# Polynomial attention and expert block on one core: first query rows in a second queue, their first factor ahead of the key projection, a shorter decode, 1e-6 added by a product, and eight warm-up matmuls for ten

## Chip, cores, metric

One core of one Trainium2 chip. The metric is the device time of one execution in microseconds (us). All quoted runs of the program on its one core are in the state called fast; a single core shows no die to compare.

In the profile's lines the first number is the start in us and the second the length. PE is TensorE's matmuls and PEld its weight loads, DVE is VectorE, ACT ScalarE, POOL GpSimd and SP SyncE; a q behind a name marks an instruction of that engine's sequencer, such as the issue of a transfer. `out<-in` names the tiles, L193 a line of the kernel, and a bracket the idle time before and what ended it.

## The reference, cut to what matters

```python
q, k, v: (4, 4, 1088, 32) float32;  S1, S2: (8, 32) float64
phi(x) = outer(S1 x, S2 x)                  # 64 features
kv = phi(k)^T v;   z = sum(phi(k))
attn = (phi(q) kv) / (phi(q) z + 1e-6)      # -> x (4352, 128)
p = domain_probs / (sum(domain_probs) + 1e-9)
out = sum_e p[:, e] * relu(x @ w1[e]) @ w2[e]   # 4 experts, 1024 wide
```

The expert block is nearly all of the work. The attention of the first 128 rows has to be ready before it can begin; the rest of the attention is fed in between its products.

## The kernel before: the parts that matter

S1 and S2 are 64-bit floats, decoded by integer operations on VectorE. Then `start()` makes the first 128 rows of x as fast as it can. Cuts are marked.

```python
load_rows(k, 0, "kn")                     # 544 KB, SyncE
load_rows(q, 0, "qn", slice(0, P))        # 64 KB, SyncE
vn[0] = load_v(0)                         # six transfers, SyncE
...
keep_warm(10)                             # products of zeros
... # words: 14 operations, then the transpose into s_T
... # ScalarE: four copies sk<-s_T; GpSimd: three sp<-s_T, four sr<-sp
def start():
    for r in range(3): key_turn(b, r)     # VectorE: kT
    qT = query_turn(b, 0, n)              # VectorE
    key_project(b, 0..2)                  # PE: sk x kT, 72 instructions
    for i in range(3): ...                # PE: factors sr[i] x qT, 24
    ...                                   # products, key sums (72), kvz
    first = attend_first(b, 0, n, qp)     # den, num; then the division
```

Later rows of x take another way: VectorE makes a tile, SyncE writes it to DRAM in four transfers (`xd<-y`) and, after waiting for these, reads it back transposed (`xT<-xd`).

## Time and profile before

| | before |
|---|---|
| time, three first runs | 491.32 us median (491.18 to 491.34); a fourth, beside the changed kernel, 491.93 |
| time, 30 further runs beside the experiments | 491.16 to 492.34, mean 491.66 |
| span of the profiled run | 489.5 us |
| first matmul of the expert block (h<-xT) | 14.16 us |

The prediction shows the lines of the page, of the chain and of VectorE's timeline.

### The profile page before, as it was taken

Reading aid. Unit: us, or ns where it says so; the run is one execution under the profiler, and the core shown is the slowest. Engines: PE = TensorE matmul, PEld = TensorE weight load, DVE = VectorE, ACT = ScalarE, POOL = GpSimd, SP = SyncE. Lnnn points to the kernel's source line nnn. Section 1 sums busy time; section 2 is a strip of 40 time slices with the busy share of each in tenths; the row PEclk is TensorE's granted clock in tenths of the full one; section 3 lists DMA queues with packets and bytes.
Section 4 is the critical chain, followed back from the end, with each engine's and each line's share of the span. In section 5 each row is a group of like instructions: output and inputs, shape, how many; then the busy total and the mean of one; then the engine's idle time right before and its main releaser. Section 6 shows DMA issues by size and latency. Waiting matters only on the chain.

```text
span 489.5 us, 11439 instructions
## 1 busy us (share of the span) xinstructions
PE 482.6 (99%) x4602; PEld 361.1 (74%) x4602; DVE 318.5 (65%) x746; ACT 244.4 (50%) x487; POOL 226.8 (46%) x260
## 2 busy tenths in 40 slices
PE   8999999999999999999999999999999999999997
PEld 5877777777767777555777777777777777878997
DVE  6759585868676757768675564575575666665642
ACT  3344463455445634535455464445455455566651
POOL 6052473516355444334555353444555355555570
PEclk9999999999999999999999999999999999999999
DMA  7990230040102520041102200031101200120000
GB/s 207 290 284 22 88 95 1 2 137 1 34 2 80 139 55 1 1 118 23 33 2 87 50 0 1 2 87 23 33 1 55 49 1 1 50 50 2 15 3 18
DMA packets 37588, 26.25 MB, mean 54 GB/s; under 512 B 26016, under 2 KB 34592, under 8 KB 37024
## 3 DMA queue, kind: packets, MB, share of 16 engines
q1 hardware_dynamic: 37520, 25.53, 19.0%
q8 instruction: 36, 0.59, 0.5%
q14 instruction: 16, 0.13, 0.1%
q10 hardware_dynamic: 16, 0.00, 0.0%
HBM read 21.28 MB, written 4.24 MB: 52 GB/s over the span
## 4 chain that ended last, share of the span: by engine, by line
PE 96%; DVE 2%; DMA 1%; issue 0%; ACT 0%; SPq 0%; DVEq 0%
PE h L188 49%; PE o L188 40%; PE f L188 4%; PE den L188 3%; DMA kn<-in_k_dram 1%; DVE qp L450 1%; DVE hid L698 1%; PE num L188 1%; PE h L176 0%; DVE kT L314 0%; ACT hid L723 0%; DVE qa L584 0%; ACT sh L842 0%; SPq L119 0%; DVE xT L486 0%
## 5 line engine op out<-in xcount | busy, mean ns | idle before, releaser
L188 PE MATMUL h<-xT,w_sb 128*64 128x512 f32 (+4 forms) x1408 | 300.2, 495 | 0.5 <-DVE xT L486 0.5
L698 DVE SCALAR_TENSOR_TENSOR hid<-h,hid 128x256 f32<-128x256 f32 (+6 forms) x432 | 203.6, 472 | 148.2 <-ACT hid L723 139.2
L723 ACT ACTIVATE hid<-h 128x512 f32<-128x512 f32 (+3 forms) x288 | 158.4, 550 | 195.0 <-PE h L188 157.0
L188 PE MATMUL o<-hid,w2s 128*64 128x256 f32 (+3 forms) x1152 | 221.6, 355 | 0.0
L188 PE MATMUL o<-hid,w_sb 128*64 128x256 f32 (+3 forms) x864 | 183.9, 355 | 0.0
L188 PEld LDWEIGHTS h<-xT,w_sb 128*64 128x64 f32 x1408 | 144.2, 137 | 51.8 <-issue 9.2
L188 PEld LDWEIGHTS o<-hid,w2s 128*64 128x64 f32 x1152 | 131.7, 137 | 30.9 <-issue 0.2
L838 POOL TENSOR_TENSOR ev<-yz,sh 64x256 f32<-64x256 f32 (+3 forms) x72 | 48.4, 672 | 163.5 <-ACT sh L841 160.8
L188 PEld LDWEIGHTS o<-hid,w_sb 128*64 128x64 f32 x864 | 101.0, 137 | 24.5 <-issue 6.3
L826 POOL TENSOR_TENSOR yz<-ev 128x512 f32<-128x512 f32 (+3 forms) x36 | 42.1, 1170 | 61.8 <-ACT ev L829 61.8
L838 POOL TENSOR_TENSOR ct<-ev 128x512 f32<-128x512 f32 (+3 forms) x36 | 42.0, 1167 | 2.8
L838 POOL TENSOR_TENSOR ct<-ct,gate 128x512 f32<-128x512 f32 (+3 forms) x27 | 32.1, 1189 | 2.1
L838 POOL TENSOR_TENSOR total<-total,ct 128x512 f32<-128x512 f32 (+3 forms) x27 | 31.8, 1179 | 2.1
L450 DVE TENSOR_TENSOR qp<-qa,qb 64x384 f32<-64x384 f32 (+3 forms) x44 | 32.1, 729 | 1.0
L828 ACT COPY ev<-o 128x512 f32<-128x512 f32 (+3 forms) x36 | 19.4, 539 | 11.3 <-PE o L188 10.8
L188 PE MATMUL o<-w_sb,hid 128*64 128x128 f32 x256 | 21.7, 273 | 0.0
L829 ACT COPY ev<-o 128x512 f32<-128x512 f32 (+3 forms) x36 | 19.4, 539 | 2.6
L715 ACT ACTIVATE hid<-h 128x256 f32<-128x256 f32 x24 | 9.2, 384 | 21.2 <-PE h L188 20.7
L188 PEld LDWEIGHTS o<-w_sb,hid 128*64 128x64 f32 x256 | 17.8, 137 | 2.1 <-issue 1.9
L353 DVE TENSOR_TENSOR kp<-fs 128x256 f32<-128x256 f32 (+1 forms) x24 | 14.7, 617 | 0.0
L841 ACT COPY sh<-yz 64x256 f32<-64x256 f32 (+3 forms) x36 | 13.7, 379 | 1.7 <-POOL yz L826 0.8
L842 ACT COPY sh<-yz 64x256 f32<-64x256 f32 (+3 forms) x36 | 13.7, 380 | 0.9
(113 smaller groups left out, 230.2 us busy)
## 6 DMA issues: line engine op xcount, KB each, us to landing
w_sb<-in_moe_w_dram SPq DMA_DIRECT2D x8, 512.0 KB, 7.5
gate<-gates SPq DMA_DIRECT2D x4, 1024.0 KB, 5.5
kn<-in_k_dram SPq DMA_DIRECT2D x4, 544.0 KB, 4.6
vn<-in_v_dram SPq DMA_DIRECT2D x16, 128.0 KB, 4.2
gate<-gates SPq DMA_DIRECT2D x2, 896.0 KB, 5.7
qn<-in_q_dram SPq DMA_DIRECT2D x3, 544.0 KB, 5.5
xd<-y SPq DMA_DIRECT2D x26, 48.0 KB, 1.7
out_dram<-ob SPq DMA_DIRECT2D x16, 64.0 KB, 2.0
```

Of the source, the lines that this page charges most:

```text
L188: nc.tensor.matmul(out(s), weights(s), moving(s), **flags)
L353: eng.tensor_tensor(out=_ap(kps[b], 0, P, 256 * t0 + P * p + 64 * x, [[256, n], [32, 2], [R, 4], [1, R]]), in0=_ap(src, 0, P, off + 4 * x, ...
L450: nc.vector.tensor_tensor(out=qp[p][64 * x : 64 * x + 64, 0:n], in0=qa[64 * p : 64 * p + 64, 0:n], in1=qb[64 * p : 64 * p + 64, 0:n], op=A ...
L698: nc.vector.scalar_tensor_tensor(out=out, in0=src, scalar=0.0, in1=in1, op0=ALU.max, op1=ALU.subtract)
L715: nc.scalar.activation(hd[:, 0 : 2 * n], hp[:, 0 : 2 * n], ACTF.Relu)
L723: nc.scalar.activation(hd[:, n * j : n * j + n], hp[:, 0:n], ACTF.Relu)
L826: add = lambda out, in0, in1, op=ALU.add: nc.gpsimd.tensor_tensor(out=out, in0=in0, in1=in1, op=op)
L828: nc.scalar.copy(_ap(ev, 0, P, 0, [[2 * w, 2], [1, w]]), _ap(a0, 0, P, 0, two))
L829: nc.scalar.copy(_ap(ev, 0, P, w, [[2 * w, 2], [1, w]]), _ap(a1, 0, P, 0, two))
L838: add = lambda out, in0, in1, op=ALU.add: nc.gpsimd.tensor_tensor(out=out, in0=in0, in1=in1, op=op)
L841: nc.scalar.copy(sh[HP:P, 0:w], yz[0:HP, 0, 0:w])
L842: nc.scalar.copy(sh[0:HP, 0:w], yz[HP:P, 1, 0:w])
```

## The change

Intent: fill the PE's wait for the keys with the first of three query factors, for which q's rows and the decoded words must come earlier; shorten the division by one operation. Two of the ten warm-up matmuls, products of zeros that raise the PE's clock, are dropped as well.

```diff
-    load_rows(q, 0, "qn", slice(0, P))
+    load_rows(q, 0, "qn", slice(0, P), nc.scalar)
...
-    keep_warm(10)
+    keep_warm(8)
... # words: shift and OR in one operation (scalar_tensor_tensor), 14 -> 12
... # copies: factor i = sp[i] on GpSimd, sr[i] two on ScalarE, two on GpSimd;
    # order: factors(0), sk (two and two), factors(1), factors(2)
@@ attend_first
+        if c == 0:
+            for _ in range(2):
+                on_side(den, ones of vx, eps, start=True, stop=False)   # 1e-6
...
-                    start=True,
+                    start=(i > 0 or c > 0),
...
-        rc = dT * 1.0 + 1e-6 ; reciprocal(rc)
+        reciprocal(rc, dT)                                    # for c == 0
@@ start
+        qT = query_turn(b, 0, n)          # before the keys
         for r in range(3):
             key_turn(b, r)
-        qT = query_turn(b, 0, n)
+        factor(0)
         key_project ...                   # second copy fs before the first of vx
+        factor(1)
+        factor(2)
```

More of the change, by code (lines that the diff above doesn't have):

```diff
@@ L84, in psum, with load_rows @@
         return pool.tile([P, 512], F32, tag=tag, name=tag)
-    def load_rows(src, b, name, part=slice(0, S)):
+    def load_rows(src, b, name, part=slice(0, S), engine=nc.sync):
         d = kn if name == "kn" else qn
@@ L92, in load_rows @@
         c, n = part.start, part.stop - part.start
-        nc.sync.dma_start(d[b][:, part], bass.AP(src.tensor, src.offset + b * H * S * D + c, [[G * D, P], [1, n]]))
+        engine.dma_start(d[b][:, part], bass.AP(src.tensor, src.offset + b * H * S * D + c, [[G * D, P], [1, n]]))
     def load_v(b):
@@ L170 @@
         nc.gpsimd.memset(own2[32 * h : 32 * h + 32, h % 2 : h % 2 + 1], 1.0)
+    eps = cpool.tile([P, 1], F32, name="eps")
+    nc.gpsimd.memset(eps[:, :], 0.0)
+    nc.gpsimd.memset(eps[0:1, :], 1e-6)
     def keep_warm(n):
@@ L200, in bits, with either @@
         nc.vector.tensor_scalar(out=out, in0=in0, scalar1=s1, scalar2=s2, op0=op0, op1=op1)
-    def either(out, a, b):
-        nc.vector.tensor_tensor(out=out, in0=a, in1=b, op=ALU.bitwise_or)
+    def either(out, in0, s1, op0, in1):
+        nc.vector.scalar_tensor_tensor(out=out, in0=in0, scalar=s1, in1=in1, op0=op0, op1=ALU.bitwise_or)
     low = _ap(s_raw, 0, R2, 0, [[2, D]])
@@ L214, with copy_on, factors @@
     bits(s_m[:, lo], high, 31, shr, 31, shl)
+    bits(s_x[:, hi], high, 12, shl, 9, shr)
     bits(s_e[:, hi], s_f[:, hi], float(127 - 1023), ALU.add, 0.0, ALU.max)
     bits(s_e[:, lo], s_f[:, hi], float(127 - 1023 - 52), ALU.add, 0.0, ALU.max)
-    bits(s_x[:, hi], high, 12, shl, 9, shr)
-    bits(s_x[:, lo], low, 29, shr)
-    bits(s_n[:, hi], s_e[:, hi], 1.0, ALU.min)
+    either(s_x[:, hi], low, 29, shr, s_x[:, hi])
     bits(s_n[:, lo], low, 3, shl, 3, shr)
     bits(s_f[:, :], s_e[:, :], 255.0, ALU.min)
-    either(s_x[:, hi], s_x[:, hi], s_x[:, lo])
-    bits(s_e[:, :], s_f[:, :], 23, shl)
-    either(s_m[:, hi], s_x[:, hi], s_m[:, lo])
-    either(s_f[:, :], s_e[:, :], s_m[:, :])
+    either(s_m[:, hi], s_m[:, lo], 0, shl, s_x[:, hi])
+    bits(s_n[:, hi], s_e[:, hi], 1.0, ALU.min)
+    either(s_f[:, :], s_f[:, :], 23, shl, s_m[:, :])
     nc.vector.tensor_tensor(out=s_hl[0:R2, :], in0=s_n[:, :], in1=s_f[:, :].bitcast(F32), op=ALU.mult)
     nc.vector.transpose(s_T[:, :], s_hl[:, :])
-    for h in range(H):
-        nc.scalar.copy(_ap(sk, 32 * h, 32, R2 * h, [[HP, 2], [1, R2]]), _ap(s_T, 0, 32, 0, [[D, 2], [1, R2]]))
-    for i in range(3):
-        nc.gpsimd.tensor_copy(
+    def copy_on(scalar):
+        return nc.scalar.copy if scalar else nc.gpsimd.tensor_copy
+    def factors(i):
+        copy_on(False)(
             _ap(sp, 0, 32, HP * i, [[32, 2], [R, 4], [1, R]]),
@@ L239 @@
         )
+        for h in range(H):
+            copy_on(h < 2)(
+                _ap(sr, 32 * h, 32, 2 * P * i + 32 * h, [[P, 2], [1, 32]]), _ap(sp, 0, 32, HP * i, [[32, 2], [1, 32]])
+            )
+    factors(0)
     for h in range(H):
-        nc.gpsimd.tensor_copy(
-            _ap(sr, 32 * h, 32, 32 * h, [[P, 6], [1, 32]]), _ap(sp, 0, 32, 0, [[32, 6], [1, 32]])
-        )
+        copy_on(h < 2)(_ap(sk, 32 * h, 32, R2 * h, [[HP, 2], [1, R2]]), _ap(s_T, 0, 32, 0, [[D, 2], [1, R2]]))
+    factors(1)
+    factors(2)
     mask_lo = [R2 + l % R2 for l in range(32)]
@@ L460, in attend_first @@
         nd = [psum(ps_n, "den"), psum(ps_n, "num")]
+        if c == 0:
+            for _ in range(2):
+                on_side(
+                    lambda s: nd[0][half[s], 0:n],
+                    lambda s: _ap(vx, 0, P, D, [[0, HP]]),
+                    lambda s: _ap(eps, 0, P, 0, [[0, n]]),
+                    start=True,
+                    stop=False,
+                )
         for i in range(2):
@@ L474, in attend_first @@
         rc = apool.tile([P, QW // 32], F32, tag="rc", name="rc")
-        nc.vector.tensor_scalar(
-            out=rc[:, 0 : n // 32], in0=_ap(dT, 0, P, 0, [[32, n // 32]]), scalar1=1e-6, scalar2=1.0, op0=ALU.add, op1=ALU.mult
-        )
-        nc.vector.reciprocal(rc[:, 0 : n // 32], rc[:, 0 : n // 32])
+        column = _ap(dT, 0, P, 0, [[32, n // 32]])
+        if c:
+            nc.vector.tensor_scalar(
+                out=rc[:, 0 : n // 32], in0=column, scalar1=1e-6, scalar2=1.0, op0=ALU.add, op1=ALU.mult
+            )
+            column = rc[:, 0 : n // 32]
+        nc.vector.reciprocal(rc[:, 0 : n // 32], column)
         rb = apool.tile([P, UNITS[0][1]], F32, tag="rb", name="rb")
@@ L613, in start, with factor @@
         b, n = 0, UNITS[0][0]
-        kf = []
+        qT = query_turn(b, 0, n)
+        fq = [psum(ps_o, "o0"), psum(ps_o, "o1"), psum(ps_n, "num")]
+        def factor(i):
+            for j in range(2):
+                both(fq[i][:, 0:n], sr[:, i, j, :], qT[:, 0:n], start=(j == 0), stop=(j == 1))
         for r in range(3):
             key_turn(b, r)
-        qT = query_turn(b, 0, n)
-        for gi in range(3):
-            kf.append(psum(ps_h, "h"))
+        factor(0)
+        kf = [psum(ps_h, "h") for _ in range(3)]
         value = value_copy(b)
         key_project(b, 0, kf[0])
+        key_project(b, 1, kf[1])
         next(value)
-        key_project(b, 1, kf[1])
         key_project(b, 2, kf[2])
@@ L626, in start @@
             pass
-        fq = [psum(ps_o, "o0"), psum(ps_o, "o1"), psum(ps_n, "num")]
-        for i in range(3):
-            for j in range(2):
-                both(fq[i][:, 0:n], sr[:, i, j, :], qT[:, 0:n], start=(j == 0), stop=(j == 1))
+        factor(1)
+        factor(2)
         qb = apool.tile([P, QW], F32, tag="qb", name="qb")
```

## The prediction

> **What bounds the kernel now.** I read the page first, its busy shares, its line of tenths and its chain, then the waits of the PE, then the chain in order of time for the first 16 us, and last the timeline of each engine over that stretch.
>
> ```profile
> span 489.5 us, 11439 instructions
> PE 482.6 (99%) x4602; PEld 361.1 (74%) x4602; DVE 318.5 (65%) x746; ACT 244.4 (50%) x487; POOL 226.8 (46%) x260
> PE   8999999999999999999999999999999999999997
> ```
>
> The PE is busy 99% of the span and only its first and last slices (12.2 us each) have gaps. From 14.2 us on, the waits of the PE name one wait on another engine, 0.6 us in total, and the stretches 14.16 to 40 us show the PE busy for 25.84 of 25.84 us. So two things follow. What this change can win lies before 14.16 us, where the main part's first real matmul starts. And what is won there should reach the end nearly whole, since nothing after it waits for a fixed date such as a weight load: no wait of the PE names one.
>
> The front part, in the chain in order of time:
>
> ```profile
> 1.21 3.73 DMA kn<-in_k_dram
> ...
> 4.96 0.72 DVE kT L314
> 5.68 0.14 issue
> 5.82 2.32 PE h L188 x72
> 8.14 0.88 PE o L188 x16
> 9.01 0.44 PE num L188 x8
> 9.45 2.12 PE f L188 x72
> ...
> 11.66 0.30 DVE kvz L376
> 11.96 0.04 issue
> 12.01 0.44 PE den L188 x4
> ...
> 13.68 0.40 DVE xT L486
> ```
>
> The key rows land at 4.94 us, VectorE turns them (kT), the PE projects the keys (72 instructions), then makes the three query factors (16 + 8 instructions, 1.32 us), then the key sums (72), all without a gap. Then comes a string of small steps: kvz, den, and on VectorE the division, shown by its timeline:
>
> ```profile
> 12.49 0.32 DVE L472 STREAM_TRANSPOSE dT<-den 128x128 f32<-128x128 f32 x1 [0.35 <-PE den L188]
> 12.85 0.17 DVE L475 TENSOR_SCALAR rc<-dT 128x4 f32<-128x4 f32 x1
> 13.05 0.18 DVE L478 RECIPROCAL rc<-rc 128x4 f32<-128x4 f32 x1
> ```
>
> The word operations that decode S1 and S2 are **not** on this chain: they end with the transpose into s_T at 4.44 us and VectorE then stands 0.52 us until the keys land. ScalarE has sk ready at 5.44 us, the first kT is there at 5.65 us.
>
> **What the Trainium skill says.** (1) "DMA: Bandwidth & Descriptors", section "Issuing engines are not separate DMA queues": transfers of all issuers run on the same 16 engines and interleave; another issuer saves only issue time. The trace agrees with the saving: one issue on SyncE takes about 0.43 us. It also warns me: today q's 64 KB stand behind the 544 KB of keys in one queue, with a second queue they move among them. (2) "VectorE: DVE Perf Modes", section on the fixed extra latency of operations whose source is in SBUF: a small operation costs a fixed amount, not by size. The trace agrees: 16x32 words take 0.16 to 0.17 us each, 16x64 take 0.18, and independent ones start 0.09 us apart, dependent ones 0.21 to 0.25. (3) "TensorE: Matmul & The Clock Gate", Part 1: the array runs at half clock until a free-running window of about 3.4 us was busy. In the trace the warm-up matmuls start 0.43 us apart until the eighth at 4.16 us and the ninth follows after 0.30 us, so the clock came up near 4.3 us, inside the eighth. (4) "PSUM — Partial Sum Buffer", the four PSUM rules: a matmul without the starting flag adds onto what the group's first one wrote. So the 1e-6 can come in as a first product. No row of the kernel before shows that use.
>
> **The change, part by part.**
>
> *q's rows by ScalarE's queue.* ScalarE's first issue ends near 1.32 us, so q is issued at about 1.35 instead of 1.62. ScalarE's table load (1.28 us) moves back by some 0.43 us to end near 3.1; ScalarE is idle until 4.54, so this is free. SyncE's later issues, v above all, come 0.43 us earlier. Before, ScalarE waited 0.39 us for v at 7.77, so that wait goes. The price: q's 64 KB now compete with the keys. At the rate of the busiest half microsecond there (418 GB/s) 64 KB are 0.16 us. I estimate that the keys land 0.1 us later, between 0 and 0.3, at about 5.05.
>
> *The words.* Fourteen operations become twelve. Following starts, 2.47 us for the first, 0.09 each for the independent ones, about 0.25 for the last three dependent steps, I get the end of s_T at about 4.16 instead of 4.44: 0.28 us. None of it is on the path by itself; it pays for the next part.
>
> *The copies.* GpSimd's sp(0) runs 4.23 to 4.46 (0.23 as now). Then two sr copies on each of ScalarE and GpSimd, of 32x64, at the 0.17 to 0.23 us spacing that the sp and sk copies show: sr(0) is ready at about 5.0. The two sk copies per engine follow: ready at about 5.45, as today. The rest, sp(1), sp(2) and four sr copies on each engine, end near 6.7 on both, before ScalarE is needed for fs (7.01 before).
>
> *Factor 0 in front.* Eight of the 24 factor instructions leave the middle. By the chain 24 cost 1.32 us, so eight cost 0.44. In front, they need q turned. VectorE now turns q first (0.27 us for 128x128, of which the next operation sees some 0.1 to 0.2), as soon as q lands, which I put close to the keys. Then kT begins at about 5.15 rather than 4.96, ends at about 5.85, and the keys' projection starts at about **6.0** instead of 5.82. Factor 0 itself (5.4 to 5.9) fits before it. So the PE's gain is 0.44 - 0.18 = 0.26 up to the end of the factors: 6.0 + 2.12 + 0.87 = 8.99 against 9.25.
>
> *The next limit.* The second fs copy now goes ahead of the first value copy. Projection plus copy latency put fs(1) at 8.13 to 8.50 (8.31 before), the first value copy then ends at about 9.06 (8.41 before), and the key sums need it: they start at 9.15, not 8.99. ScalarE takes 0.16 of the 0.26. VectorE's products: the first at 8.6, the others after the third fs copy at 9.1, then 1.1 us of products and 1.18 us of qp, to 11.4; the key sums end at 9.15 + 2.27 = 11.42. Both about agree, so kvz starts at about 11.52 instead of 11.66: **0.14 us**.
>
> *1e-6 as a product.* The added four instructions (0.22 us at the 55 ns apart of the factors) depend on nothing late and lie between the last key sum and den, where the PE stands 0.46 us: hidden. The tensor_scalar on rc goes: the reciprocal moves from 13.05 to 12.85, **0.20 us**, wholly on the path. The four warm-up matmuls behind end at 13.65 before and, with den earlier, still before xT.
>
> *Two warm-up matmuls fewer.* They now end near 4.6 instead of 5.05, still after 4.3. The PE is then idle until about 5.4. If the clock stays up: nothing.
>
> Sum: 0.14 + 0.20 = 0.34 us, less a little for what I don't see; 491.32 - 0.32 = **491.0 us**.
>
> **Rivals.** (a) *The keys are not held up*, because the slow start of their transfer (113 GB/s until 3 us) leaves room for q. Then the projection starts at about 5.85, the sums at 9.0, and the gain is about 0.5: 490.8. For it: that slow start. Against: 418 GB/s in the half microsecond from 3.5. (b) *q lands after the keys*: now VectorE waits for q before it turns any key, a wait in place of none. q landed 3.6 us after issue before, behind the keys; at the same latency it would be 4.95, no loss, but with interleaving it could be 5.3, and the projection starts at 6.25. The factor's gain is then spent and only the 0.20 of the reciprocal stays, or less: 491.1 to 491.3. (c) *The clock is not yet up* when eight warm-up matmuls end, because the window's phase differs by execution. Then the projection runs at half speed for a while, about 1 us lost: 492. For it: only 0.2 to 0.3 us of margin after 4.3. Against: three runs within 0.16 us, so the phase looks steady, and the window that released the clock ends within the eight. (d) *The front's gain is swallowed later* by a stage with its own date, the loads of w1 and w2: they are also issued 0.4 us earlier, and the PE does not wait for them now, so I give this little; it would leave 491.3.
>
> **Range and chances.** Main case and (a) together about 70%: 490.7 to 491.1. (b) and (d) about 20%: 491.1 to 491.4. (c) about 10%: up to 492.3. The 8 in 10 range is 490.5 to 491.5. Two per cent are 9.8 us; the whole front is 14 us and the change touches some tenths of it. So within 2% has 0.98, and I leave one in a hundred for each other side.
>
> **What would show it.** Right: the first matmul of the main part (h from xT) starts at about 13.8 instead of 14.16 and the distance from there to the end is unchanged within 0.1 us; no operation between dT and the reciprocal; the den group has eight instructions, four of them before kvz is done; the eight factor instructions lie between 5.3 and 5.95; the keys land at 5.0 to 5.1 and the projection starts at about 6.0; the sums start behind the first value copy at about 9.1. Wrong: VectorE's wait before the first turn names q and ends after 5.1 (rival b); the projection's 72 instructions take over 2.5 us (rival c); the start of h moves but the span does not (rival d); or the eps products run after kvz and delay den.

## The result

The changed kernel took 492.64 us in the median of four runs (492.14 to 493.03), and 492.24 to 493.61 in five later ones. Ratios here are the mean time of one kernel's fast runs over that of the other's of the same rounds, so not quite the ratio of the medians: 1.0024, 95% interval 1.0006 to 1.0041, and 1.0029 (1.0016 to 1.0042) the second time. Within 2%, as given 0.98, but **longer by 1.2 us in the first mean and 1.5 us in the second, where 0.3 us less was forecast**, and outside the range.

The page after, top lines, and the chain in order of time:

```profile
span 490.5 us, 11449 instructions
PE 483.0 (98%) x4604; PEld 360.7 (74%) x4604; DVE 318.8 (65%) x743; ACT 245.1 (50%) x491; POOL 227.6 (46%) x266
```

```profile
5.88 0.66 PE o L193 x8
6.54 2.25 PE h L193 x72
8.79 0.44 PE o L193 x8
9.23 0.44 PE num L193 x8
9.67 2.25 PE f L193 x72
...
12.01 0.30 DVE kvz L388
...
12.36 0.44 PE den L193 x4
...
13.82 0.38 DVE xT L510
14.21 0.13 DVE kvx L399
14.34 0.11 issue
14.45 1.53 PE h L193 x24
```

Factor 0 (o, eight instructions) is in front, as planned, but the projection begins at about 6.5 us (5.82 before); the chain reaches h at 14.45 us, 0.29 later. VectorE's timeline shows what it waited for:

```profile
5.42 0.31 DVE L455 STREAM_TRANSPOSE qT<-qn 128x128 f32<-128x128 f32 x1 [1.22 <-DMA qn<-in_q_dram]
5.66 1.26 DVE L326 STREAM_TRANSPOSE kT<-kn 128x512 f32<-128x512 f32 x2
...
13.20 0.18 DVE L502 RECIPROCAL rc<-dT 128x4 f32<-128x4 f32 x1
```

q landed at 5.40 us; the keys, by the trace's semaphore records, at 5.12 (4.94 before). So VectorE stood with the keys in hand and waited for q. SyncE waited as well, by its waits over the first 20 us:

```profile
SPq L140 <- DMA qn<-in_q_dram: 1.0, 1, 1.0
```

The program keeps eight semaphores for such transfers and hands them out in turn; the transfer eight places behind q's reuses q's and must wait for it. Before the change the transfer at that point reused the semaphore of the keys, which landed at 4.94. SyncE's later issues move back accordingly: the first weights go out at 7.80 us, not 7.41.

This makes a second wait at h. xT ended at 14.21 us (14.06 before), and in the other traces but e2's h begins 0.10 to 0.11 us after xT ends; here it begins 0.24 after. The chain names `kvx`, but the first weights landed at 14.31 us (13.55 before) and the PE's weight load follows at 14.42. So of the 0.29 us about 0.15 are the late front and 0.14 the late weights. The other 0.62 us of this run are lost at one place 120 us later. Timelines there, before:

```profile
131.22 0.34 SPq L558 DMA_DIRECT2D xT<-xd  x1
...
133.75 1.94 PE L188 MATMUL h<-xT,w_sb 128*64 128x512 f32 x8
```

and after:

```profile
132.04 0.34 SPq L582 DMA_DIRECT2D xT<-xd  x1
...
134.66 1.94 PE L193 MATMUL h<-xT,w_sb 128*64 128x512 f32 x8 [0.43 <-DVE hid L725]
```

The PE stalls where a new chunk of x begins. The profile names VectorE as the releaser, but the matching record is the landing of xT: 134.41 us, with the PE's weight load at 134.63. Before, it was 133.50 and 133.72. The same 0.22 us in both: this stage was **bound by that landing already**, with so little lost that no view showed it. The ScalarE operations of the expert block, paired one by one between the traces, run 0.29 us late from 15 to 130 us and 0.91 us late from 136 us to the end.

Two things then stay unexplained by this one trace: why SyncE issued that read 0.49 us after the last landing it waited for (131.55 to 132.04; before, 131.12 to 131.22), and why some runs took 0.7 to 1.4 us more than others.

### The profile page after: what moved, and what is told of

It is laid out like the page before. It is cut to its first block, busy times and chain, and to the rows that moved or that the text cites. A ratio compares the mean times of both kernels' runs of the same rounds, so it can differ in the third digit from the quotient of the medians.

```text
span 490.5 us, 11449 instructions
## 1 busy us (share of the span) xinstructions
PE 483.0 (98%) x4604; PEld 360.7 (74%) x4604; DVE 318.8 (65%) x743; ACT 245.1 (50%) x491; POOL 227.6 (46%) x266
## 4 chain that ended last, share of the span: by engine, by line
PE 95%; DVE 2%; issue 0%; DMA 0%; ACT 0%; POOL 0%; DVEq 0%; ACTq 0%
PE h L193 48%; PE o L193 40%; PE f L193 4%; PE den L193 3%; DVE hid L725 1%; DVE qp L462 1%; PE num L193 1%; DMA s_raw<-in_S_dram 0%; ACT hid L750 0%; PE h L181 0%; DVE qa L608 0%; DVE qb L603 0%; POOL sp L242 0%; POOL sr L247 0%; ACT sh L869 0%
```

## The experiments

Five rounds each unless noted. "Difference" is the mean of the runs less the mean of the kernel before that is recorded with the job.

| run | times, us | mean | difference |
|---|---|---|---|
| e1 changed kernel again | 492.24 to 493.61 | 493.10 | +1.48 |
| e2 old order at the start | 491.93 to 493.81 | 492.45 | +0.83 |
| e3 q by SyncE | 491.41 to 493.63 | 492.71 | +1.09 |
| e4 both | 491.21 to 492.77 | 491.68 | +0.06 |
| e5 ten warm-up matmuls | 492.02 to 492.64 | 492.27 | +0.65 |
| e6 one more SyncE transfer | 491.97 to 493.49 | 492.56 | +0.94 |
| e7 1e-6 product alone | 491.46 to 492.47 | 491.81 | +0.19 |
| e8 front delayed (3 rounds) | 491.74 to 492.08 | 491.94 | +0.32 |
| e9 keys issued first | 493.95 to 494.33 | 494.17 | +2.48 |
| e10 back part only | 491.25 to 492.12 | 491.62 | -0.07 |
| e11 as e9, one transfer fewer (four runs) | 493.32 to 494.62 | 493.95 | +2.26 |
| e12 q by SyncE, ten warm-ups | 491.30 to 491.71 | 491.49 | -0.20 |
| e13 extra transfer, ten warm-ups | 491.51 to 491.92 | 491.77 | +0.08 |

The runs with eight warm-up matmuls (the changed kernel, e1 to e4, e6) fall into a short and a long group, so their means also tell how many runs fell into the long one.

My theory after the first trace had three parts: A, the front waits for q, and the weights come later; C, the clock gate; E, SyncE's position in its instructions. Rivals: the stall near 134 us is a matter of the run (B), the order alone matters (D), the second queue itself delays later issues (F), a late front misses the date (G).

**e1, the changed kernel unchanged.**

> The changed kernel unchanged, to see its spread. Theory A (q's rows land after the keys and VectorE waits for them; the first weights land later; and the transposed queries of the chunk at 134 us come 0.6 us late): the fastest runs at 492.1 to 492.3, main part starting at 14.4 us, a stall of the PE near 134 us in this trace as well. Rival B (chance: the stall near 134 us is a matter of the run): some of five runs near 491.6, and the trace without the stall. Rival C (phase of the clock gate): a second group of runs some 0.7 us longer, with a lower mean clock, whatever else.

The stall near 134 us is there again (SyncE's issue 0.49 us behind the last landing), so B falls. And the profiled run fell into the long group. Its PE timeline:

```profile
1.19 3.59 PE L181 MATMUL h<-warm 128*128 128x512 bf16 x8 [1.19 <-DVE s_hl L218]
5.86 1.12 PE L193 MATMUL o<-qT,sr 128*64 128x128 f32 x8 [1.08 <-DVE qT L455]
6.74 3.30 PE L193 MATMUL h<-sk,kT 128*64 128x64 f32 x72
```

Factor 0 took 1.12 us instead of 0.66 and the projection 3.30 instead of 2.32: half clock. In this trace the full clock was granted at 8.97 us, by the trace's clock records; in the first trace of the changed kernel at 5.42.

**e2, old order at the start.**

```diff
-        qT = query_turn(b, 0, n) ; keys ; factor(0) ; ...
+        keys ; qT = query_turn(b, 0, n) ; projection ; factors 0..2
```

> The changed kernel with the old order at the start: keys turned and projected first, then the query factors; q still in ScalarE's queue. Theory A: the keys land near 5.1 us as in the changed kernel, are turned at once, projection at 6.0, xT at 14.0, but w1 lands at 14.3 as in the changed kernel, because SyncE's next issue waits for q's landing at 5.4; so h starts at 14.4 and the time does not fall, 492.1. Rival D (only the order matters, the queue costs nothing): h starts at 13.9 to 14.1 and the time is 491.1 to 491.3, or 0.6 more if the stall near 134 us stays.

The projection began at 5.89 us and h at 14.30. Its waits name the cause:

```profile
PE h L193 <- DMA w_sb<-in_moe_w_dram: 0.6, 1, 0.6
```

So with q in ScalarE's queue, the weights become the date that binds h, as theory A said; making the front faster would not have helped there. D falls. The stall near 134 us stayed.

**e3, q by SyncE, factor 0 in front.**

```diff
-    load_rows(q, 0, "qn", slice(0, P), nc.scalar)
+    load_rows(q, 0, "qn", slice(0, P))
```

> The changed kernel with q's first rows back in SyncE's queue, factor 0 still in front. Theory A: keys land at 4.94, q at 5.2, VectorE turns q from 5.2 and the keys from 5.46, projection at 6.25, w1 lands at 13.55 as before, h starts at 14.05; 491.2 without and 491.8 with the stall near 134 us. Rival D: as the changed kernel, 492.2.

Two runs at 491.41 and 491.48, four at 493.0 to 493.6: the expected short time and a long group. The profiled run was of the long group (clock granted at 10.08 us):

```profile
5.71 1.12 PE o L193 x8
6.83 3.63 PE h L193 x72
```

SyncE's issue near 133 us came 0.10 us behind the last landing.

**e4, both undone.** The diffs of e2 and e3 together.

> The changed kernel with both undone: q by SyncE and the old order at the start; what stays is the words, the shared copies, 1e-6 as a product and eight warm-up matmuls. Theory A: projection at 5.8 as before, the reciprocal 0.2 us earlier, h starts at 13.9 to 14.0, 491.1 without and 491.7 with a stall near 134 us. Rival C (eight warm-up matmuls are too few): projection slower than 2.4 us in some runs, a group near 492.

h at 14.02 us, four runs at 491.2 to 491.6, and one at 492.77: eight warm-up matmuls without anything else of the front.

**e5, ten warm-up matmuls.**

```diff
-    keep_warm(8)
+    keep_warm(10)
```

> The changed kernel with ten warm-up matmuls as before in place of eight. Theory C (the clock gate's window is at another phase in each execution, and eight matmuls end too early for some phases): the group of runs above 492.6 goes, all runs within 491.9 to 492.7, the projection of the keys takes under 2.5 us; what stays is the changed kernel's fast group, 492.2. Rival (the slow group comes from the late queries or from another stage): a group near 493.3 stays.

The range is 492.02 to 492.64 and the mean falls by 0.82 us against e1, which ran in another job (the kernel before had a mean of 491.62 us in both). Theory C holds. Its timeline, for comparison with e1:

```profile
1.19 3.73 PE L181 MATMUL h<-warm 128*128 128x512 bf16 x10 [1.19 <-DVE s_hl L218]
6.02 0.66 PE L193 MATMUL o<-qT,sr 128*64 128x128 f32 x8 [1.10 <-DVE qT L455]
6.62 2.32 PE L193 MATMUL h<-sk,kT 128*64 128x64 f32 x72
```

Over all traces: with ten matmuls the grant came at 3.89 to 6.53 us in seven of seven (the kernel before, e5, e7, e8, e10, e12, e13). With eight, at 5.07 to 5.42 in three (the changed kernel, e2, e4) and at 8.97 to 10.23 in three (e1, e3, e6); the first three profiled runs are of the short group of their kernels and the last three of the long one. By time alone, 14 of the 30 runs with eight are in a long group. (e9 and e11 have ten too, but a longer gap; see there.)

**e6, one more transfer by SyncE.**

```diff
         load_w2(e)
+    nc.sync.dma_start(spare, 512 numbers of domain_probs)   # read by nothing
```

> The changed kernel with one more small transfer issued by SyncE behind the weights (512 numbers into a tile that nothing reads), so that SyncE has as many issues as before the change. Theory E (with one issue fewer SyncE reaches the end of its fetched instructions at another place, and its issue of the transposed queries comes 0.49 us after the last landing instead of 0.10): the delay is 0.10 again, the stall near 134 us falls from 0.6 to 0.1 us, the 8 KB instruction transfer stands before that issue; fast group 491.7. Rival F (the delay comes from the two queues or from the semaphores): the stall stays, 492.2.

SyncE's issue came 0.02 us after the last landing and the stall near 134 us was gone (ScalarE's operations behind it run 0.16 us ahead of those of the kernel before, counted from the block's start). But two of five runs had the late clock, and the three others, 491.97 to 492.04, were only some 0.2 us under the changed kernel's short group, not 0.6. Inconclusive in time; e13 repeats it with the clock mended.

**e7, the 1e-6 product alone, on the kernel before.**

> The kernel before with only the 1e-6 as a product. Theory A: den unmoved, reciprocal 0.2 us earlier, h starts at 13.95, w1 is there at 13.55 so it does not bind; span 0.1 to 0.2 us shorter than before: 491.0 to 491.7 over the runs, with the spread of before. Rival (w1 or the queries at 134 us take it back): as before within 0.05 us.

From the start of kvz to h: 12.02 to 14.32, so 2.30 us, against 2.50 before. The part gives its 0.20 us. The run's time does not show it: the keys landed at 5.29 us in this trace (4.94 before) with nothing changed about them, and the mean is within the spread. So 0.2 us of gain and 0.35 us of landing chance lie side by side.

**e8, the front delayed and nothing else.**

```diff
-        nc.vector.transpose(dT, nd[0])
+        twice for c == 0
```

> The kernel before with the first transpose of den made twice: a delay of about 0.35 us in front and nothing else. If a later front by itself makes the queries late near 134 us (rival G), the time rises by 0.35 plus 0.6 to 492.4; theory E: by 0.35 alone, 491.9, and SyncE's issue stays 0.10 us behind the last landing.

The block began 0.42 us later in the trace and ended 0.42 us later; SyncE's issue stayed 0.10 us behind the last landing. G falls: everything moves together and the date moves too.

**e9, e10, e11: can a better version be had?** e9 keeps the words, the shared copies (sk first) and the product, restores the old order and ten warm-ups, and has both S1 and S2 in ScalarE's queue so that SyncE issues the keys first; with the extra transfer. e10 is e4 with ten warm-ups. e11 is e9 without the extra transfer.

> Words, shared copies (sk before the factors' copies) and the 1e-6 product of the change, old order at the start, ten warm-up matmuls; S1 and S2 both in ScalarE's queue, so that SyncE issues the keys first, at 0.74 us, and one small extra transfer behind the weights, so that SyncE's number of issues is that of before. Keys should land at 4.5, the words end at 4.75, the projection start near 5.55, h near 13.7; mean some 0.4 us under the kernel before, about 491.2. Rival: the words become the bound and end later than 5 us (S2 lands late in ScalarE's queue), no gain.

> What stays of the change when its front part and the two removed warm-up matmuls are undone: words, shared copies, 1e-6 as a product; q by SyncE, old order, ten warm-up matmuls. Theory: 0.1 to 0.2 us under the kernel before in the mean, 491.4, with no run above 492.3. Rival: no difference that shows in the spread of the landing of the keys.

> The first of these three without the extra transfer, so SyncE has one issue fewer than before the change, for another reason than q. Theory E: SyncE's issue of the transposed queries near 131 us comes 0.5 us behind its last wait again, PE stalls some 0.5 us near 134 us more than in the first, time 491.7. Rival F (q's transfer in ScalarE's queue was the reason): no such delay, as the first.

e9 lost 2.5 us. The 2 KB of S2, issued at 1.35 us in the second queue, landed at 5.01 us among the keys (2.37 before). The PE then idled for over 2 us after the warm-ups and the clock was withdrawn, seen in the profile's windows (the columns are the stretch, its length, then busy time of PE, PEld, DVE, ACT, POOL, then PEclk, DMA share and GB/s):

```profile
4.50:8.00 3.50, 1.17 (x20) 0.63 (x20) 2.82 (x16) 0.83 (x4) 0.98 (x5) 0.99 0.73 136
8.00:11.40 3.40, 3.40 (x68) 3.40 (x65) 1.15 (x5) 2.44 (x9) 2.57 (x9) 0.50 0.96 301
11.40:14.80 3.40, 3.40 (x99) 3.36 (x96) 2.41 (x10) 0.98 (x4) 2.84 (x12) 1.00 1.10 353
```

The clock's records here: full from 4.55, half from 7.96, full from 11.37 us. The late S2 costs without that too: e11's profiled run kept the full clock from 5.72 us on and began the projection at 7.75 us (5.82 before), and took 493.32 us. e10 is level with the kernel before; its trace has a later landing near 131 us and a 0.4 us delay of the PE near 24 us (also in e5's trace) that I did not follow up. e11, which has one SyncE issue fewer for another reason than q, has SyncE's 0.48 us pause between its last wait and its issue again, so F falls as the only reason. Its time doesn't show it: the PE had no stall there. My expected half microsecond was not seen because the last write landed some 0.5 us earlier (counted from the block's start) than in the kernel before.

**e12 and e13, with the clock mended.** e12 is e3 with ten warm-ups, e13 is e6 with ten.

> The change with q by SyncE and ten warm-up matmuls: words, shared copies, 1e-6 product and factor 0 in front stay. If the clock's phase is the whole of the slow group of the run with q by SyncE, no run lies above 492.4 now. The front then costs what its fast group shows: VectorE waits for q to 5.2, projection at 6.3, less 0.44 of factors and 0.20 of the reciprocal: 491.4 to 491.7, at or just under the kernel before. Rival (factor 0 in front loses by itself): 492.0 or more.

> The changed kernel with ten warm-up matmuls and the extra transfer by SyncE, so with the clock and SyncE's position both mended, q still in ScalarE's queue. Theory E with C: the stall near 134 us is 0.2 us at most and SyncE's pause of 0.48 us is not between its last wait and its issue; mean 491.6 to 491.8, against 492.27 with ten warm-up matmuls alone. Rival F: 492.2 as with ten warm-up matmuls alone.

In e12 the long group is gone: 491.30 to 491.71. q landed late here too:

```profile
5.42 0.31 DVE L455 STREAM_TRANSPOSE qT<-qn 128x128 f32<-128x128 f32 x1 [1.39 <-DMA qn<-in_q_dram]
```

so the front still starts late and gains nothing; h began at 14.31 us. In e13 the stall near 134 us is gone and the mean is 0.08 us over the kernel before, 0.57 us less by that measure than e5. The two traces agree in the place: from 130 to 136 us e5's lost 0.38 us against the kernel before and e13's gained 0.16. But e5's trace also has the unexplained delay near 24 us (0.33 us of it stays), which e13's lacks.

## Why the prediction was wrong, by its own steps

These are its steps and what the runs showed.

- **"Two warm-up matmuls fewer. If the clock stays up: nothing."** This step failed most. It was read from one trace in which the clock came up at 4.33 us. The moment is not the kernel's: e9's three records are 3.41 us apart, and the first grants of other traces, divided by 3.41, leave remainders all over that range: 0.48 us in e7, 1.24 in e12, 2.31 in e11, 3.26 in e3. A window that ends too empty grants nothing, and the next end is 3.41 us off. The eight matmuls end at about 4.8 us by the timeline. In the changed kernel's first trace the window from 2.01 to 5.42 held 2.77 us of them (81%) and the clock was granted; in e1 the one from 2.14 to 5.55 held 2.64 (77%) and it was not. In e7's, from 0.48 to 3.89, 2.70 (79%) sufficed. (The windows' starts are an estimate from the recorded ends less 3.41, and the matmuls' ends are modelled.) Mean cost: 0.82 us, the changed kernel again against e5. This was rival (c), given a tenth; three of six traces had it. It is not the whole of the miss: the changed kernel's short group, 492.14 to 492.31 us, still lies outside the range.
- **"What is won there should reach the end nearly whole, since nothing after it waits for a fixed date."** Wrong twice. The weights bound h, by 0.14 us in the changed kernel's first trace and 0.26 in e2, which is rival (d) in part. And the chunk at 134 us was bound by the landing of its transposed queries already. A wait of 0.2 us behind a landing, hidden among matmul ends, had no line in the waits of the PE. It is no fixed date (e8: it moves with the block), but a start won in front is not safe behind it: in e4's trace h began 0.14 us early and 0.03 us of that were left after 136 us, where that landing took 2.38 us from its issue (2.28 before). Cost in the first trace 0.62 us; e13 against e5, with the extra SyncE transfer, recovers 0.57.
- **"VectorE turns q first, as soon as q lands, which I put close to the keys."** The keys at 5.12 were right (5.05 forecast, and 0 to 0.3 us of delay; over all traces but e9's and e11's the keys landed at 5.16 us on average with q in ScalarE's queue and 5.00 with q in SyncE's, with ranges that overlap), q at 5.40 was not. kT began at 5.66, not 5.15, and the projection at 6.47, not 6.0. That is rival (b). In SyncE's queue it was turned hardly sooner (e12: 5.42, e3: 5.25), so this wait comes from turning q first; the queue costs through the later weights.
- **"SyncE's later issues, v above all, come 0.43 us earlier."** The transfers of v did; those behind it came 0.4 us later, for the reuse of q's semaphore. This is the step that made the weights late. I had not looked up which transfer's semaphore each later issue waits for.
- **The words.** s_T ended at 4.20 us (4.16 forecast). Right, and worthless, since VectorE then stood 1.22 us.
- **The copies.** The first factor's were ready at 5.06 us (5.0 forecast). Right.
- **"The next limit":** not reached; behind the late projection the key sums began at 9.55 us (9.15 forecast).
- **1e-6 as a product:** kvz to the end of xT took 2.19 us (12.01 to 14.21) against 2.40 (11.66 to 14.06). 0.20 us, right; the added products ran before kvz was done.

The mean loss of 1.48 us (e1) thus divides, by the steps e1 to e5 to e13 to e12, into 0.82 for the clock, 0.57 for the date at 134 us, and 0.28 for q's queue, with 0.20 left as a gain; the last two are of the size of the spread. The first job's four runs lost 1.17 us in the mean: two of these four lie in the long group, against four of five in e1. e12 is the best version: 0.9996 of the kernel before, interval 0.9983 to 1.0008, so not shown to be better.

**What stays open.** SyncE pauses once for 0.47 to 0.48 us near this place. In the five traces with 62 issues before that read (the changed kernel, e1, e2, e5, e11) the pause lies between its last wait and the issue; in the traces with 63 the issue follows the last wait by 0.08 to 0.17 us (in e6, e9 and e13 the issue itself waits too, and follows the last landing by 0.02), and in three of them (e6, e7, e12) the pause can be seen between its two last waits. An 8 KB transfer of instructions starts 0.62 to 0.64 us after the end of each visible pause. In the seven traces without a visible one it starts 1.07 to 1.23 us after the first of the two waits, as it would if the pause lay there, hidden in the second wait. So by the transfer's date the pause stands one instruction earlier in every trace with 63 issues. That it is a fetch is argued from this position, not shown. The extra transfer also shifts which semaphore each write uses, so e13 doesn't separate the two entirely.

## What to carry to other kernels

Warm-up matmuls are dimensioned for the worst phase of the clock's window, not for the phase of one trace; look at several traces, and count the long group before and after. Before calling a stage bound by compute, compare the landing of each input with the first use: a constant short distance in two traces (here 0.22 us) suggests that the transfer sets the date. When an issue is moved between queues, count what moves with it: the semaphores that later issues wait for, and the position of the waiting issue itself; and do not put a small urgent transfer beside a large one in another queue in the hope that it passes (2 KB took until 5.01 us, 64 KB until 5.40).

## What the Trainium skill lacked or had wrong

- "TensorE: Matmul & The Clock Gate", Part 1, says that the window is free-running, 3.41 us long, and that the transition varies by some 500 ns. The length agrees (4.55, 7.96, 11.37 us in e9). The variation does not: with ten matmuls, begun at 1.19 us, the grant came at 3.89 to 6.53 us, and with eight, which end at 4.8, at 5.07 to 10.23. It lacks how full a window must be: here 79% and 81% sufficed and 77% did not, by modelled ends. Its advice in "Why this matters for your kernels", at least 4 us of matmuls, is the side that the runs support.
- "DMA: Bandwidth & Descriptors", "Issuing engines are not separate DMA queues", says that another issuer only saves issue time. The trace agrees that data interleave (in the changed kernel's first trace the DMA engines finish their shares of the keys from 4.42 to 5.12 us and those of q from 4.64 to 5.40), but the section lacks two costs: a small transfer beside a large one can finish with it or after it (2 KB issued at 1.35 us landed at 5.01; 64 KB at 5.40, after the 544 KB at 5.12), and, in a program that reuses its semaphores in turn, issues elsewhere can inherit a wait for it (SyncE 1.0 us).
- "Runtime: NRT & Kernel Launch" has a section on instruction fetch, but neither it nor another page has a pause like SyncE's of 0.48 us at one place in its instructions, which moves by one instruction when an issue is taken away. If it is a fetch, it belongs there.
- "PSUM — Partial Sum Buffer", the four PSUM rules: the first product's value was kept and added onto, and all kernels that use it were correct. Nothing lacked.
